# Stores of the last group in fewer transfers over two queues, and sums and weightings moved behind a bank's read, in a fused linear-attention and SwiGLU kernel

## The chip, the cores and the metric

The kernel runs on one core of one Trainium2 chip. The metric is the device time of one execution in microseconds (us), the median over several runs. A profile is one execution with the hardware profiler on; its "span" runs from the first to the last instruction and is about 2 us shorter than the device time. The record gives each run a state, fast or slow; all runs named here were fast, so like is compared with like.

## The reference

Eight batch entries of 576 tokens with eight heads of width 64 go through a linear attention, whose output (4608 tokens of width 512) goes through a gated feed-forward layer of inner width 1536.

```python
def _attn_ref(q, k, v):                      # q, k, v: (8, 8, 576, 64)
    theta = pi / 2 * arange(S) / S
    phi = lambda x: concatenate([relu(x) * cos(theta), relu(x) * sin(theta)], axis=-1)
    q_p, k_p = phi(q), phi(k)
    kv = einsum('bhsf,bhsd->bhfd', k_p, v)
    z = sum(k_p, axis=2)
    return einsum('bhsf,bhfd->bhsd', q_p, kv) / (einsum('bhsf,bhf->bhs', q_p, z)[..., None] + 1e-6)

def _moe_ref(x, w_gate, w_val, w_out):       # x: (4608, 512), weights 512x1536, 512x1536, 1536x512
    g = x @ w_gate
    return (g * sigmoid(g) * (x @ w_val)) @ w_out
```

## The kernel before

The 4608 tokens are worked in nine groups of 512. For each group TensorE runs 12 steps of the first two matmuls (line 531). Between them it makes the attention tiles of the next group, which are transposed by DMA into `xT`. From the third group on, the last matmul of a group is done as seven products on half-size blocks (Strassen's way), in `out_by_quarters`. Each product is 12 matmuls of 256 columns (line 640), and is added up in a "bank", a buffer of partial sums that VectorE or ScalarE reads (`a`, `b`, `c`, `e` in the code). Four token sums of the hidden tile (line 611) feed the products; weight differences were made once.

In this section code is cut; "# ..." marks a cut.

```python
def store(t, cols=slice(0, d_model), queues=None):          # two transfers, 64 partitions each
    for e in range(2):
        idx = 2 * t + e
        (queues or (nc.sync, nc.sync))[e].dma_start(out=out_v[idx // NC, idx % NC][:, cols],
                                                    in_=ob_of(t)[e * SH:(e + 1) * SH, cols])

def sums_behind(fc):                                         # token sums, some after each step
    for n, lo, hi in {7: ((3, 0, 4),), 8: ((1, 0, 4),), 9: ((2, 0, 4),), 10: ((4, 0, 4), (3, 4, 6)),
                      11: ((1, 4, 6), (2, 4, 6), (4, 4, 6))}.get(fc, ()):
        token_sum(n, lo, hi)

def phi_q(b, g):                                             # one "weighting": relu, then times a table
    # ...
    relu_op("act", o, o)                                                      # ScalarE, line 234
    nc.vector.tensor_tensor(out=st[b, "q"][:, g], in0=..., in1=tab, op=ALU.mult)   # VectorE, line 251

def out_by_quarters(tg, slot_of):
    # ... product(to, a, b, first) is 12 matmuls; added(o, ps, x) is VectorE: o = ps * DOWN + x  (line 647)
    product(a, aq[:, 0, 0], bq[:, 0, 0], True)               # 1st
    nc.scalar.mul(out=C12, in_=a[0], mul=DOWN)
    product(e, S3, T3, True)                                 # 2nd
    added(C22, e, C12)
    # ...
    slot_of(0)                                               # other work: a weighting
    product(b, S2, T2, True)                                 # 3rd, into bank b
    added(C21, b, C22)                                       # reads b
    product(a, aq[:, 1, 0], bq[:, 1, 0], False)              # 4th
    nc.scalar.mul(out=C11, in_=a[0], mul=DOWN)
    # ... last group: store C11
    slot_of(1)                                               # a weighting
    product(b, S1, T1, False)                                # 5th, adds onto bank b
    added(C22, b, C22)                                       # reads b
    # ... last group: store C22
    product(c, aq[:, 1, 1], T4, True)                        # 6th
    added(C21, c, C21)
    # ... store C21 (last group) or the two lower tiles
    slot_of(2)                                               # a weighting
    product(b, S4, bq[:, 1, 1], False)                       # 7th, adds onto bank b
    added(C12, b, C12)
    # ... store C12 (last group) or the two upper tiles
    slot_of(3)

def load_behind(b):                                          # GpSimd: loads start when phit has landed
    nc.gpsimd.tensor_copy(out=hold2, in_=phit[b - 1][0:1, :, 0, 0, 0])
    load(b, "q")
    if b > 3:
        load_kv(b)

# which slot takes which weighting (b > 3): four of q, then four of k and v; qturn_dma (SyncE) turns q into phit
fs, tq = [p0 + 11 + i for i in range(8)], (p0 + 15, p0 + 16)
```

## Time and profile before

| | before |
|---|---|
| device time, median of the first three runs | 323.78 us (323.49 to 324.77) |
| span of the profiled run | 321.0 us |
| TensorE busy | 309.1 us (96%) |
| holes (idle time) of TensorE at products, by its weight loads | 2.7 us, in four groups |
| the tail: last add to the output tile, to the end of the span | 7.5 us |

A line of the timeline gives the start in us, the duration in us, the engine, the source line, the operation and its tiles; in brackets stands how long the engine was idle just before, and what ended that. PE is TensorE's matmuls, PEld its weight loads, DVE VectorE, ACT ScalarE, POOL GpSimd; L640 is line 640 of the kernel. "SPq" and "ACTq" are DMA issues on the queues of SyncE and ScalarE. In a list of waits the numbers are the total in us, the count and the longest; "issue" there means that the profile names no cause. The prediction below shows the lines of this profile.

### The profile page before, as it was taken

How to read it: one execution, taken by the hardware profiler on the slowest of the kernel's cores; microseconds unless marked ns; L12 is line 12 of the kernel's file. 1: busy time of each engine (PE TensorE's matmuls, PEld its weight loads, DVE VectorE, ACT ScalarE, POOL GpSimd, SP SyncE). 2: the span in 40 equal slices, each digit the busy share in tenths (PEclk: the TensorE clock that was granted, in tenths of full speed). 3: DMA queues.
4: the chain of work that ended last, by engine and by line, in shares of the span. 5: the costliest groups of instructions: out<-in, count | busy, mean ns of one | idle time of the engine just before them, and what ended most of it. 6: DMA issues, size and time to landing. Idle time of an engine off the chain costs nothing.

```text
span 321.0 us, 6625 instructions
## 1 busy us (share of the span) xinstructions
PE 309.1 (96%) x2624; PEld 182.9 (57%) x2624; DVE 224.8 (70%) x448; ACT 130.1 (41%) x237; POOL 35.3 (11%) x60
## 2 busy tenths in 40 slices
PE   8899999999999989999999999999999999999990
PEld 4596555454445574558554855476547644854580
DVE  7873876788658888598859875888487448643750
ACT  7553556662436345334433543244431132223210
POOL 6755102010102000020003000300000000000000
PEclk9999999999999999999999999999999999999997
DMA  7999998988996956999696959597931411150014
GB/s 266 216 200 198 205 202 143 211 111 109 179 203 81 195 73 148 133 124 166 140 133 97 198 132 135 78 182 155 143 63 33 98 34 34 35 130 3 0 26 104
DMA packets 74862, 41.06 MB, mean 128 GB/s; under 512 B 50000, under 2 KB 69968, under 8 KB 74832
## 3 DMA queue, kind: packets, MB, share of 16 engines
q1 hardware_dynamic: 52480, 22.95, 40.2%
q0 software_dynamic: 22192, 17.57, 36.6%
q8 instruction: 20, 0.33, 0.4%
q10 hardware_dynamic: 160, 0.13, 0.2%
q14 instruction: 10, 0.08, 0.1%
HBM read 37.75 MB, written 9.44 MB: 147 GB/s over the span
## 4 chain that ended last, share of the span: by engine, by line
PE 75%; DVE 10%; DMA 5%; issue 3%; SPq 3%; ACT 2%; DVEq 0%; POOLq 0%; POOL 0%; ACTq 0%
PE banks L531 49%; PE banks L640 13%; PE banks L580 6%; DMA phit<-r_q 3%; PE banks L301 2%; DVE ob L647 2%; DMA raw_q<-in_q_dram 2%; DVE ht L542 2%; DVE sums L611 2%; PE banks L415 1%; SPq L570 1%; SPq L274 1%; DVE r_q L251 1%; PE banks L461 1%; PE banks L397 1%
## 5 line engine op out<-in xcount | busy, mean ns | idle before, releaser
L537 ACT ACTIVATE sg<-banks 128x512 bf16<-128x512 f32 (+2 forms) x116 | 65.8, 568 | 120.1 <-PE banks L531 113.1
L531 PE MATMUL banks<-xT,wv_sb 128*128 128x512 bf16 (+2 forms) x464 | 111.3, 364 | 0.0
L531 PE MATMUL banks<-xT,wg_sb 128*128 128x512 bf16 (+2 forms) x464 | 111.3, 364 | 0.0
L542 DVE TENSOR_TENSOR ht<-sg,banks 128x512 f16<-128x512 bf16 (+2 forms) x116 | 74.5, 648 | 51.7 <-PE banks L531 44.7
L531 PEld LDWEIGHTS <-wv_sb 128*128 128x128 bf16 x464 | 44.9, 98 | 48.7
L531 PEld LDWEIGHTS <-wg_sb 128*128 128x128 bf16 x464 | 43.1, 98 | 41.7 <-issue 0.2
L640 PEld LDWEIGHTS <-ht 128*128 128x128 f16 x336 | 32.4, 98 | 6.6 <-issue 2.7
L647 DVE SCALAR_TENSOR_TENSOR ob<-banks,ob 128x512 f32<-128x512 f32 (+1 forms) x38 | 24.5, 647 | 13.6 <-PE banks L640 13.5
L640 PEld LDWEIGHTS <-sums 128*128 128x128 f16 x252 | 24.6, 98 | 2.9
L255 DVE TENSOR_TENSOR v<-raw_v,tab 128x1152 bf16<-128x1152 bf16 x31 | 22.7, 752 | 0.2 <-ACT raw_v L691 0.2
L580 PE MATMUL banks<-wo_sb,ht 128*128 128x512 f16 x96 | 22.7, 379 | 0.0
L438 DVE TENSOR_TENSOR x<-banks,rec 128x512 bf16<-128x512 f32 (+1 forms) x32 | 21.6, 674 | 1.3 <-PE banks L397 0.3
L251 DVE TENSOR_TENSOR r_q<-raw_q,tab 128x1152 bf16<-128x1152 bf16 x24 | 17.9, 753 | 5.2 <-ACT raw_q L234 5.2
L640 PE MATMUL banks<-wt_sb,ht 128*128 128x256 f16 x168 | 19.5, 272 | 2.0 <-DVE ob L647 2.0
L640 PE MATMUL banks<-wo_sb,ht 128*128 128x256 f16 x168 | 20.6, 273 | 0.0
L640 PE MATMUL banks<-wt_sb,sums 128*128 128x256 f16 x168 | 19.5, 273 | 0.0
L234 ACT ACTIVATE raw_k<-raw_k 128x576 bf16<-128x576 bf16 (+1 forms) x25 | 17.0, 694 | 0.0
L234 ACT ACTIVATE raw_q<-raw_q 128x576 bf16<-128x576 bf16 x24 | 15.4, 675 | 2.5 <-DMA raw_q<-in_q_dram 2.5
L611 DVE TENSOR_TENSOR sums<-ht 128x1024 f16<-128x1024 f16 (+1 forms) x28 | 15.5, 553 | 0.2
L840 POOL COPY hold<-phit 1x2 bf16<-1x2 bf16 x5 | 0.9, 176 | 132.5 <-DMA phit<-r_q 132.5
L580 PEld LDWEIGHTS <-ht 128*128 128x128 f16 x96 | 9.1, 98 | 8.9 <-issue 0.2
L415 PEld LDWEIGHTS <-phit 128*128 128x128 bf16 (+1 forms) x240 | 10.0, 100 | 6.5 <-issue 1.3
(95 smaller groups left out, 210.5 us busy)
## 6 DMA issues: line engine op xcount, KB each, us to landing
out_dram<-ob SPq DMA_DIRECT2D x64, 128.0 KB, 2.4
raw_k<-in_k_dram POOLq DMA_DIRECT2D x7, 576.0 KB, 9.0
raw_q<-in_q_dram POOLq DMA_DIRECT2D x6, 576.0 KB, 6.6
raw_v<-in_v_dram POOLq DMA_DIRECT2D x6, 576.0 KB, 12.2
wo_sb<-in_moe_w_out_dram POOLq DMA_DIRECT2D x3, 512.0 KB, 12.8
wg_sb<-in_moe_w_gate_dram POOLq DMA_DIRECT2D x5, 256.0 KB, 9.0
wv_sb<-in_moe_w_val_dram POOLq DMA_DIRECT2D x5, 256.0 KB, 9.4
wo_sb<-in_v_dram SPq DMA_DIRECT2D x2, 576.0 KB, 4.1
```

The costliest lines, as they stand in the source:

```text
L234: nc.scalar.activation(out=out, in_=in_, func=AF.Relu)
L251: nc.vector.tensor_tensor(out=st[b, "q"][:, g], in0=o.unsqueeze(2).to_broadcast([P, NC, 2, D]), in1=tab, op=ALU.mult)
L255: nc.vector.tensor_tensor(out=v2s[b % 2][:, g, :, :, 0:D], in0=(first if b == 0 and g == 0 else {"v": raw_of(b, "v")})["v"][:, g].unsqueez ...
L415: nc.tensor.matmul(out=ps[ms, e, g * D1:(g + 1) * D1], lhsT=phit[b][:, e, g, c:c + n].rearrange("p c s -> p (c s)"), rhs=kv2s[b % 2][:, e, ...
L438: nc.vector.tensor_tensor(out=st["x", t].rearrange("p (y e d) -> p e y d", e=2, d=D)[:, :, ys], in0=ps[:, :, 0:2 * J * D1].rearrange("p e ...
L531: nc.tensor.matmul(out=st["f", tg, fc, lo][i], lhsT=(wg_sb, wv_sb)[i][:, kc, fs], rhs=xT[tg][:, ts, kc], start=(kc == 0), stop=(kc == KC - 1))
L537: nc.scalar.activation(out=sg[:, 0:n], in_=st["f", tg, fc, lo][0], func=AF.Silu, scale=DOWN)
L542: nc.vector.tensor_tensor(out=ht[:, fc, r:r + n], in0=st.pop(("s", tg, fc, lo))[:, 0:n], in1=ps[1], op=ALU.mult)
L580: nc.tensor.matmul(out=o_ps[t], lhsT=ht[:, fc, r:r + P], rhs=wo_sb[:, fc], start=(fc == 0), stop=(fc == FC - 1))
L611: nc.vector.tensor_tensor(out=o[:, lo:hi], in0=x[:, lo:hi], in1=y[:, lo:hi], op=op)
L640: nc.tensor.matmul(out=at_of(to, i), lhsT=a[:, kc, i * P:(i + 1) * P], rhs=b[:, kc], start=first and kc == 0 and (i == 0 or len(to) == 2), ...
L647: nc.vector.scalar_tensor_tensor(out=o[:, sl], in0=ps[i][:, 0:1] if len(ps) == 2 else ps[i], scalar=DOWN, in1=x[:, sl], op0=ALU.mult, op1= ...
```

## The change

It intends two things. In the last group, whose stores nothing hides, it makes fewer store instructions and shares them between SyncE and ScalarE. In the groups that also weight the next batch entry, it takes a token sum and two weightings out of VectorE's way ahead of the read that the fifth product waits for.

```diff
+    def store_two(t, cols):
+        for e in range(2):
+            (b, c), (b1, _) = divmod(2 * t + e, NC), divmod(2 * t + 2 + e, NC)
+            assert b == b1
+            (nc.sync, nc.scalar)[e].dma_start(
+                out=out_v[b, c:c + 3:2, :, cols].rearrange("c p f -> p c f"),
+                in_=obs[t // 2][e * SH:(e + 1) * SH, :, cols])
 # ... sums_behind
-                          11: ((1, 4, 6), (2, 4, 6), (4, 4, 6))}.get(fc, ()):
+                          11: ((1, 4, 6), (2, 4, 6))}.get(fc, ()):
 # ... out_by_quarters
-        slot_of(0)
         product(b, S2, T2, True)
         added(C21, b, C22)
+        token_sum(4, 4, 6)
+        slot_of(0)
         product(a, aq[:, 1, 0], bq[:, 1, 0], False)
 # ... the last group's first three quarters (one of them shown)
         if last:
-            for t in (t0, t0 + 1):
-                store(t, slice(0, HD))
+            store_two(t0, slice(0, HD))
 # ... the plan of the weightings
-            fs, tq = [p0 + 11 + i for i in range(8)], (p0 + 15, p0 + 16)
+            fs, tq = [p0 + 12, p0 + 12] + [p0 + 11 + i for i in range(2, 8)], (p0 + 15, p0 + 16)
```

The last quarter, C12, is stored as before in four 64 KB transfers, two on each queue.

More of the change, by code (lines that the diff above doesn't have):

```diff
@@ L671, in out_by_quarters @@
         if last:
-            for t in (t0 + 2, t0 + 3):
-                store(t, slice(HD, d_model))
+            store_two(t0 + 2, slice(HD, d_model))
         c = home("c")
@@ L677, in out_by_quarters @@
         free("c")
-        for t in (t0 + 2, t0 + 3):
-            store(t, slice(0, HD) if last else slice(0, d_model))
+        if last:
+            store_two(t0 + 2, slice(0, HD))
+        else:
+            for t in (t0 + 2, t0 + 3):
+                store(t)
         slot_of(2)
@@ L684, in out_by_quarters @@
         for t in (t0, t0 + 1):
-            store(t, slice(HD, d_model) if last else slice(0, d_model), (nc.sync, nc.scalar) if last else None)
+            store(t, *((slice(HD, d_model), (nc.sync, nc.scalar)) if last else ()))
         slot_of(3)
```

## The prediction

> **What bounds the kernel now.** I read the page's first two parts, then the lists of waits, then the timeline around the seven-product output of each group (line 640 is every product, line 647 the VectorE operation that adds a bank into the output tile, line 251 a weighting of q, line 611 a token sum), and last the timeline of the end.
>
> ```profile
> span 321.0 us, 6625 instructions
> PE 309.1 (96%) x2624; PEld 182.9 (57%) x2624; DVE 224.8 (70%) x448; ACT 130.1 (41%) x237; POOL 35.3 (11%) x60
> PE   8899999999999989999999999999999999999990
> ```
>
> TensorE is the bound: every slice is full but the last and the start. So only two things can pay: holes in TensorE's row, and the part after its last matmul. 321.0 less 309.1 is 11.9 us. The list of waits says where the holes lie (columns: total us, times, longest):
>
> ```profile
> PE banks L640 <- DVE ob L647: 2.0, 4, 0.9
> PEld L640 <- issue: 2.7, 4, 1.1
> ```
>
> There are four holes, all at products and all ended by VectorE. The weight-load row counts 2.7 us, since a matmul's modelled end hides some of the gap. In the timeline one such hole (fourth group) looks so:
>
> ```profile
> 145.85 0.42 DVE L611 TENSOR_TENSOR sums<-ht,sums 128x512 f16<-128x512 f16 x1
> 146.19 0.75 DVE L251 TENSOR_TENSOR r_q<-raw_q,tab 128x1152 bf16<-128x1152 bf16 x1
> ...
> 147.92 0.69 DVE L647 SCALAR_TENSOR_TENSOR ob<-banks,ob 128x512 f32<-128x512 f32 x1
> 148.07 1.47 PE L640 MATMUL banks<-wo_sb,ht 128*128 128x256 f16 x12
> 148.52 0.75 DVE L251 TENSOR_TENSOR r_q<-raw_q,tab 128x1152 bf16<-128x1152 bf16 x1
> 149.19 0.68 DVE L647 SCALAR_TENSOR_TENSOR ob<-banks,ob 128x512 f32<-128x512 f32 x1
> 149.58 0.60 ACT L663 ACTIVATE ob<-banks 128x512 f32<-128x512 f32 x1 [2.76 <-PE banks L640]
> 149.93 2.78 PE L640 MATMUL banks<-wt_sb,ht 128*128 128x256 f16 x24 [0.39 <-DVE ob L647]
> 150.07 1.25 ACT L234 ACTIVATE raw_q<-raw_q 128x576 bf16<-128x576 bf16 x2
> 150.78 0.76 DVE L251 TENSOR_TENSOR r_q<-raw_q,tab 128x1152 bf16<-128x1152 bf16 x1 [0.90 <-ACT raw_q L234]
> 151.45 0.68 DVE L647 SCALAR_TENSOR_TENSOR ob<-banks,ob 128x512 f32<-128x512 f32 x1
> 152.54 1.47 PE L640 MATMUL banks<-wo_sb,sums 128*128 128x256 f16 x12
> ```
>
> The fourth product starts at 148.07. The fifth adds onto the bank that VectorE's read at 149.19 has yet to take out, and starts at 149.93, when that read ends. VectorE is late because a token sum and two weightings stand ahead of it. The end of the kernel:
>
> ```profile
> 309.16 0.60 ACT L663 ACTIVATE ob<-banks 128x512 f32<-128x512 f32 x1 [3.33 <-PE banks L640]
> 309.78 8.79 SPq L570 DMA_DIRECT2D out_dram<-ob  x14
> 311.58 1.47 PE L640 MATMUL banks<-wo_sb,sums 128*128 128x256 f16 x12
> 312.93 1.44 ACTq L570 DMA_DIRECT2D out_dram<-ob  x2
> 313.09 0.42 DVE L647 SCALAR_TENSOR_TENSOR ob<-banks,ob 128x256 f32<-128x256 f32 x1 [0.23 <-PE banks L640]
> ```
>
> The results are complete at 313.51 (313.09 + 0.42), but SyncE is still issuing its 14 stores until 318.57, one every 8.79 / 14 = 0.63 us. The last one starts at 318.0 and takes 2.0 us from issue to landing (median of these 14), so 320.0; the span ends 1.0 us later. The tail is bound by one queue's issuing.
>
> **What the Trainium skill says.** (1) "Perfetto Trace Analysis", section "What 'DMA-bound' means": a kernel can be bound by the issuing engine's sequencer, seen as a solid row of DMA slices there. The trace agrees: 14 issues without a hole while the DMA engines are at 0.28 to 0.75 of their time in each microsecond from 313 to 320. (2) "DMA: Bandwidth & Descriptors", section "Issuing engines are not separate DMA queues": issuing from several engines saves only the sequencer's time for issuing. Here that time is the bound, so it is just what counts. (3) Same page, "Anatomy of one DMA": about 2.0 us fixed per DMA, mostly the receipt of the write. The trace has 1.9 to 2.3 us for the last 16 stores. (The page fitted it for another issuing path; the trace's figure is the one I use.) (4) "PSUM — Partial Sum Buffer", "The four PSUM rules": a synchronised read of a partial sum in the midst of accumulation is allowed. That is what the bank does between third and fifth product, and the wait at 149.93 is the synchronisation.
>
> **The change, part by part.** TensorE's instruction order is the same; only VectorE, ScalarE and the stores differ. (I compared the built orders.)
>
> *Stores.* Last group: 16 transfers of 64 KB become six of 128 KB and four of 64 KB, half on each queue, so SyncE issues 5 and not 14. Nothing is saved in bytes. When do they go out, if nothing before the tail moved? First pair at 309.78, second at 310.9 (after the add at 310.47), third pair after the add at 311.78, which takes about 0.6: 312.4. The last four need the two adds that end at 312.9 and 313.51. At 0.6 us an issue: 312.4 to 313.0, 313.0 to 313.65, 313.65 to 314.3 on SyncE. ScalarE's two old issues take 0.55 and 0.79 (1.44 in all with a gap), so there I have the last start at 313.7 to 313.8. Is a doubled transfer dearer to issue? The first loads of the run, on SyncE, have 128 rows of two pieces each and take 0.44 to 0.51 us to issue, so I take no more than 0.6 to 0.7. Landing: 2.0 on SyncE, 2.3 on ScalarE (its median). I add 0.1 because 512 KB now leave within 1.3 us; at 179 GB/s with a share of 0.75 (microsecond 314 to 315) full rate is about 240 GB/s, so 512 KB need 2.1 us of the engines and the last pieces queue a little. So landing at about 316.1 and not 320.0: **minus 3.9 us** (3.6 to 4.2).
>
> *Moved work.* One token sum (0.42) and two weightings (0.75 each, 0.67 from start to start) leave the place before the third bank's read; a third weighting was behind it already. Only the groups that carry weightings (the four with holes) gain. Without the hole the fifth product starts 1.31 after the fourth (246.84 to 248.15 in a later group without weightings), so the holes are: 117.18 − 114.79 − 1.31 = 1.08; 149.93 − 148.07 − 1.31 = 0.55; and by the same sum 0.51 and 0.53. Together 2.67, the 2.7 of the list. But the work does not vanish. In the new order VectorE has, for the fourth group: read of the third product at 148.27 (0.20 after its end) to 148.87, token sum to 149.29, two weightings to 150.63. The third weighting still needs ScalarE's relu at 150.07, which waits for ScalarE's copy of the fourth product: it starts at 150.78 as before. Then the read after the fifth product starts at 151.45, as before, and ends at 152.13. The **seventh** product adds onto that bank too. TensorE would reach it at 148.07 + 3 × 1.31 = 152.00 and waits until 152.19. So a new wait of 0.19 remains, and the group gains 152.54 − 152.19 = 0.35, not 0.55. The same sum gives 0.88 for the first such group (read 118.17 to 118.86, seventh at 118.92 for 119.80), then 0.31 and 0.32. Sum: **minus 1.86 us**. The rest of the run is full on TensorE, so it reaches the end.
>
> Total 3.9 + 1.86 = 5.8; 323.78 − 5.8 = **318.0 us**, 1.8% less.
>
> **The rivals.** *A: the moved work comes back entire at the seventh product.* For it: three weightings stand in a row. Against: the last is paced by ScalarE as before. It would leave the tail alone: 319.9. *B: no wait comes back,* as when products run a bit later or the adds release sooner: 2.67 and 3.9 give 317.2, the only way past 2%. *C: the tail becomes bound by DMA bandwidth or by dearer issues.* Two 128 KB transfers at a time at 240 GB/s need 1.1 us a quarter and quarters come 1.1 to 1.5 us apart, so it is near the limit; if the two-piece stores took 1.2 us each to issue, the last landing moves by about 0.6 and the total to 318.6. *D: later weightings delay the transposes and loads behind them.* The last weighting of a group comes no later than before, so I see nothing.
>
> **Range and chances.** Tail 3.4 to 4.3, moved work 1.2 to 2.7, runs that scatter by some 0.5 us (323.49 to 324.77 before): 316.9 to 319.3. Faster by over 2% needs 6.5 us, nearly the whole of B with the best tail: 0.2. Slower has no mechanism: 0.01.
>
> **What would show it.** In the new profile: five store issues on each of SyncE and ScalarE; last store issued about 2.2 us before landing and within 0.4 us of the last add; last add to span's end about 3.6 us (7.5 before). No wait at the fifth product; four waits of about 0.2 us at the seventh. Last matmul about 1.9 us earlier. Wrong if the seventh waits as long as the fifth did, if a two-piece store takes over 1 us to issue, or if landing takes over 3 us.

## The result and the profile after

| | before | after |
|---|---|---|
| device time, median (lowest to highest), four runs each | 323.63 (323.12 to 324.77) us | 318.36 (318.19 to 318.71) us |
| ratio | | 0.983, 95% interval 0.981 to 0.986 |
| span of the profiled run | 321.0 us | 316.5 us |
| holes of TensorE at products | 2.7 us | 0.8 us |
| idle time of TensorE before the sixth group, by its weight loads | 0.2 us | 0.8 us |
| last add to the end of the span | 7.5 us | 4.2 us |

A ratio is the mean time of one kernel's fast runs over that of the other's in the same rounds, so it is not quite the ratio of the medians. The device time fell by 5.3 us, where 5.8 were predicted.

The page's first lines after:

```profile
span 316.5 us, 6619 instructions
PE 308.6 (98%) x2624; PEld 182.7 (58%) x2624; DVE 225.0 (71%) x448; ACT 130.1 (41%) x237; POOL 35.7 (11%) x60
PE   8899999999999999999999999999999999999994
```

Busy times hardly changed (TensorE 308.6 us for 309.1); TensorE's share rose since the span shrank around it, and the last slice now holds work. From the list of waits after (line 640 has become 648):

```profile
PEld L648 <- issue: 0.8, 4, 0.2
PEld L531 <- issue: 0.8, 1, 0.8
PE banks L531 <- DMA xT<-x: 0.6, 1, 0.6
```

The four holes at products are down from 1.1 at most to 0.2 each. (A wait in the start-up, at L372, is also longer, 0.8 us for 0.2; the first group with a gain still starts its products only 0.05 us later.) A wait for a DMA has come up: once, TensorE comes to a group's first step and the transposed input has not landed. The fourth group's products in the timeline after (line 647 is now 655, 611 is 619, 663 is 672):

```profile
147.23 1.47 PE L648 MATMUL banks<-wo_sb,ht 128*128 128x256 f16 x12
147.43 0.69 DVE L655 SCALAR_TENSOR_TENSOR ob<-banks,ob 128x512 f32<-128x512 f32 x1 [0.56 <-PE banks L648]
148.04 0.41 DVE L619 TENSOR_TENSOR sums<-ht,sums 128x512 f16<-128x512 f16 x1
148.37 1.42 DVE L251 TENSOR_TENSOR r_q<-raw_q,tab 128x1152 bf16<-128x1152 bf16 x2
148.54 2.78 PE L648 MATMUL banks<-wt_sb,ht 128*128 128x256 f16 x24
148.74 0.60 ACT L672 ACTIVATE ob<-banks 128x512 f32<-128x512 f32 x1 [2.19 <-PE banks L648]
149.24 1.25 ACT L234 ACTIVATE raw_q<-raw_q 128x576 bf16<-128x576 bf16 x2
149.94 0.76 DVE L251 TENSOR_TENSOR r_q<-raw_q,tab 128x1152 bf16<-128x1152 bf16 x1 [0.15 <-ACT raw_q L234]
150.62 1.43 DVE L655 SCALAR_TENSOR_TENSOR ob<-banks,ob 128x512 f32<-128x512 f32 x2
151.36 1.47 PE L648 MATMUL banks<-wo_sb,sums 128*128 128x256 f16 x12
```

The fourth product starts at 147.23, and the fifth at 148.54, 1.31 later and without a hole: VectorE now reads the bank at 147.43, at once. The sum and two weightings come after that read. The third weighting waits for ScalarE's relu, and the next read of the bank starts only at 150.62. The seventh product starts at 151.36, 2.82 after the fifth, where 2.62 would be free of waiting: the 0.2 us that are left.

Where the new wait shows, at the start of the sixth group:

```profile
183.98 1.47 PE L648 MATMUL banks<-wo_sb,sums 128*128 128x256 f16 x12
185.98 0.56 PEld L531 LDWEIGHTS <-wg_sb 128*128 128x128 bf16 x4 [0.82 <-issue]
186.01 1.02 PE L531 MATMUL banks<-xT,wg_sb 128*128 128x512 bf16 x4 [0.56 <-DMA xT<-x]
```

And the same place in the kernel before:

```profile
186.90 0.56 PEld L531 LDWEIGHTS <-wg_sb 128*128 128x128 bf16 x4 [0.23 <-issue]
```

After the change the group's last transpose was issued at 178.61, 2.4 us earlier than before (181.0), since VectorE reaches that tile sooner. But it took 7.3 us to land where it had taken 5.8, and landed at 185.88. In the kernel before it landed at 186.79. In both kernels the first weight load of the group starts 0.10 us after the landing, so TensorE waited for this transpose before the change too: 0.2 us, where the other groups from the fourth on start with 0.01 us of idle time. The list of waits of before has it as `PEld L531 <- issue: 0.2, 1, 0.2`, with no DMA named, and the prediction passed over it.

The tail after:

```profile
308.54 3.31 SPq L577 DMA_DIRECT2D out_dram<-ob  x3
308.54 3.35 ACTq L577 DMA_DIRECT2D out_dram<-ob  x3
...
311.84 0.42 DVE L655 SCALAR_TENSOR_TENSOR ob<-banks,ob 128x256 f32<-128x256 f32 x1 [0.23 <-PE banks L648]
311.94 1.20 SPq L570 DMA_DIRECT2D out_dram<-ob  x2
311.99 1.44 ACTq L570 DMA_DIRECT2D out_dram<-ob  x2
```

Both queues issue at the same times. The output is complete at 312.26 (311.84 + 0.42), and the last issue starts at 312.87 on ScalarE, 0.6 us later; on the one queue before it started 4.5 us after the last add.

### The profile page after: what moved, and what is told of

The parts are those of the page before. It is cut to its first block, busy times and chain, and to the rows that moved or that the text cites. A ratio compares the mean times of both kernels' runs of the same rounds, so it can differ in the third digit from the quotient of the medians.

```text
span 316.5 us, 6619 instructions
## 1 busy us (share of the span) xinstructions
PE 308.6 (98%) x2624; PEld 182.7 (58%) x2624; DVE 225.0 (71%) x448; ACT 130.1 (41%) x237; POOL 35.7 (11%) x60
## 4 chain that ended last, share of the span: by engine, by line
PE 92%; DMA 2%; DVE 2%; ACT 2%; issue 0%; ACTq 0%
PE banks L531 59%; PE banks L648 18%; PE banks L588 6%; PE banks L301 3%; PE banks L415 2%; DMA xT<-x 2%; PE banks L461 1%; PE banks L397 1%; DVE v L255 1%; PE banks L168 1%; PE banks L341 0%; PE banks L503 0%; ACT L200 0%; ACT phit L349 0%; ACT kvd L313 0%
## 5 line engine op out<-in xcount | busy, mean ns | idle before, releaser
L531 PE MATMUL banks<-xT,wg_sb 128*128 128x512 bf16 (+2 forms) x464 | 111.3, 364 | 0.6 <-DMA xT<-x 0.6
L531 PE MATMUL banks<-xT,wv_sb 128*128 128x512 bf16 (+2 forms) x464 | 111.3, 364 | 0.0
L531 PEld LDWEIGHTS <-wv_sb 128*128 128x128 bf16 x464 | 44.9, 98 | 48.7
L531 PEld LDWEIGHTS <-wg_sb 128*128 128x128 bf16 x464 | 43.1, 98 | 42.3 <-issue 0.8
```

Of the source, the lines that this page charges most:

```text
L531: nc.tensor.matmul(out=st["f", tg, fc, lo][i], lhsT=(wg_sb, wv_sb)[i][:, kc, fs], rhs=xT[tg][:, ts, kc], start=(kc == 0), stop=(kc == KC - 1))
```

## The experiments

The theory: the tail was bound by SyncE's issuing, and the moved work takes away the holes at the fifth product but runs into two later limits, a small one at the seventh product and the landing of the transposes of x. The rivals: merging rather than the second queue shortens the tail; the wait for the transpose is chance; what is gained ahead of a wait is not lost in it. All results were correct.

| run | time, us | ratio (95% interval) | span | last add to end |
|---|---|---|---|---|
| after_again | 318.21 | 0.984 (0.982 to 0.986) | 317.1 | 4.2 |
| stores_only | 320.15 | 0.990 (0.988 to 0.992) | 318.5 | 4.1 |
| moves_only | 321.77 | 0.995 (0.993 to 0.997) | 319.7 | 7.5 |
| two_queues_64k | 318.44 | 0.984 (0.982 to 0.986) | 316.6 | 4.1 |
| one_queue_128k | 319.87 | 0.989 (0.987 to 0.990) | 317.8 | 5.5 |
| third_later | 318.72 | 0.984 (0.982 to 0.986) | 317.1 | 4.1 |
| pairs_all | 317.29 | 0.981 (0.979 to 0.983) | 315.5 | 4.0 |
| pairs_third | 316.88 | 0.979 (0.978 to 0.981) | 315.4 | 4.0 |
| pairs_third_again | 316.80 | 0.978 (0.976 to 0.980) | 315.0 | 4.0 |
| last_merged | 316.90 | 0.979 (0.977 to 0.981) | 315.3 | 4.2 |

The kernel before had medians of 323.41 us (11 runs, the first four rows), 323.64 (9 runs, the next four) and 323.84 (9 runs, the last two).

### The changed kernel again

> The changed kernel once more, as the measure for the others of this call. Both theories: about 318.3 us (0.984 of before). What it is to tell: whether the new wait of TensorE for the transpose of x (0.7 to 0.8 us at the start of the sixth group) belongs to the kernel or was chance. If it belongs: 0.6 to 0.9 us again in the same place, last add to end of the span 4.2 us. If chance: no such wait and a span of 315.7.

The wait came again, in the same place: 1.3 us of TensorE's idle time before the sixth group. So it is not chance, but its size is not steady. Of the runs below that have the moved work and, in the earlier groups, the stores of before, each has such a wait too: 0.3 us in moves_only and in two_queues_64k, at the start of the fifth group, 0.4 us in one_queue_128k, at the start of the seventh, and three in third_later. By the weight loads TensorE is idle before the sixth group in all six of these runs (0.3 to 1.6 us), and not in stores_only (0.01 us).

### The stores alone

Edit: from the changed kernel, the moved work back in its old places.

```diff
-                          11: ((1, 4, 6), (2, 4, 6))}.get(fc, ()):
+                          11: ((1, 4, 6), (2, 4, 6), (4, 4, 6))}.get(fc, ()):
+        slot_of(0)
         product(b, S2, T2, True)
         added(C21, b, C22)
-        token_sum(4, 4, 6)
-        slot_of(0)
-            fs, tq = [p0 + 12, p0 + 12] + [p0 + 11 + i for i in range(2, 8)], (p0 + 15, p0 + 16)
+            fs, tq = [p0 + 11 + i for i in range(8)], (p0 + 15, p0 + 16)
```

> Only the stores changed; token sum and weightings in their old places. My theory: the two parts don't touch, so the tail alone comes back: last add to end 4.2 us for 7.5, four holes of 2.7 us in all still at the fifth product, no wait for the transpose; 323.6 - 3.3 = 320.3 us, ratio 0.990. Rival: if the stores owe part of their gain to the earlier end of the last group, under 2.5 us.

The time fell by 3.3 us and the tail by 3.4, as the theory had it. The holes at the fifth product were 3.5 us by the weight loads in this run, one of them 1.4: there the q that is to be weighted landed late (ScalarE stood idle for it 2.4 us, until 146.55), and in the old order that weighting stands ahead of the read.

### The moves alone

Edit: from the kernel before, the same lines as above the other way round, with the stores of before.

> Only the moved sum and weightings; the stores of before. My theory: holes at products go from 2.7 to 0.8 us, a wait of about 0.7 us for the transpose of x comes up in the sixth group, so the last matmul comes 1.2 us earlier, tail 7.5 as before: 322.4 us, ratio 0.996. Rival (the wait for the transpose is from the stores or chance): no such wait, 321.7 us.

The time fell by 1.6 us (321.77 for 323.41), between the two forecasts. The holes at products were 0.8 us and the tail 7.5, as expected; the wait for the transpose was 0.3 us and in the fifth group (by the weight loads 0.6 us there and 0.3 before the sixth), so smaller and not where it was expected. The two parts alone give 3.3 + 1.6 = 4.9 us of the 5.2 that the whole gave: within the scatter they add up.

### Two queues, not merged; merged, one queue

Edit for two_queues_64k: `store_two` issues its two rows as separate 64 KB transfers.

```diff
-            (nc.sync, nc.scalar)[e].dma_start(out=out_v[b, c:c + 3:2, :, cols]..., in_=obs[t // 2][e * SH:(e + 1) * SH, :, cols])
+            for i in range(2):
+                b, c = divmod(2 * (t + i) + e, NC)
+                (nc.sync, nc.scalar)[e].dma_start(out=out_v[b, c][:, cols], in_=obs[t // 2][e * SH:(e + 1) * SH, i, cols])
```

> The changed kernel, but the merged stores of the last group split again into 64 KB transfers, eight on each queue. Theory A (one queue's issuing was the limit, two queues remove it, and merging adds little): last store issued within 1 us of the last add, tail 4.0 to 4.6 us, time within 0.3 us of the changed kernel. Theory B (the number of transfers matters): each queue falls behind by two issues, last issue about 1.3 us later, tail 5.3 us, time about 319.4 us.

Edit for one_queue_128k: the merged stores and the last four all go to SyncE.

```diff
-            (nc.sync, nc.scalar)[e].dma_start(
+            nc.sync.dma_start(
-            store(t, *((slice(HD, d_model), (nc.sync, nc.scalar)) if last else ()))
+            store(t, *((slice(HD, d_model),) if last else ()))
```

> The changed kernel with its merged stores of the last group all on SyncE (ten issues on one queue). Theory A (one queue's issuing is the limit of the tail): the last four issues follow two of the third quarter at 0.6 us each, so the last starts about 1.9 us after the last add and not 0.6, tail 5.4 us for 4.2, time 319.5 us. Theory B (merging alone did it): tail 4.2 to 4.5 us, time 318.3 us.

Without merging but over two queues the time was 318.44 us, the changed kernel's within the scatter. The last issue came 1.1 us after the last add and not 0.6, but its 64 KB landed in 2.0 us and the span ended 1.0 us later (2.3 and 1.4 us in the changed kernel). With merging on one queue it was 319.87 us. The end of that kernel's timeline:

```profile
311.86 0.42 DVE L655 SCALAR_TENSOR_TENSOR ob<-banks,ob 128x256 f32<-128x256 f32 x1 [0.23 <-PE banks L648]
312.63 2.48 SPq L570 DMA_DIRECT2D out_dram<-ob  x4
```

The last four issues take SyncE from 312.63 to 315.11, 2.8 us beyond the last add at 312.28. So one queue's issuing time sets the tail: merging, with all ten issues on one queue (before: fourteen there and two on ScalarE's), leaves 5.5 us of 7.5, and sharing between two queues takes it to 4.1 or 4.2 with or without merging.

### The third weighting later

Edit: one more weighting goes behind the read after the fifth product.

```diff
-            fs, tq = [p0 + 12, p0 + 12] + [p0 + 11 + i for i in range(2, 8)], (p0 + 15, p0 + 16)
+            fs, tq = [p0 + 12, p0 + 12, p0 + 14] + [p0 + 11 + i for i in range(3, 8)], (p0 + 15, p0 + 16)
```

> The changed kernel with the third weighting of a group (and its relu) moved behind the read after the fifth product. My theory: the four waits of 0.2 us at the seventh product go (0.8 us to under 0.1), but TensorE then reaches the next group earlier and waits longer for the transpose of x that lands with the burst of loads: that wait grows from 0.3-1.3 us by about 0.5. Net: 318.0 us, no clear gain. Rival: the gain reaches the end in full, 317.5 us.

The holes at products were gone. TensorE's waits in the later two thirds of that run:

```profile
152.99 1.04 PE L531 MATMUL banks<-xT,wg_sb 128*128 128x512 bf16 x4 [0.42 <-DMA xT<-x]
185.99 1.02 PE L531 MATMUL banks<-xT,wg_sb 128*128 128x512 bf16 x4 [0.40 <-DMA xT<-x]
219.10 1.02 PE L531 MATMUL banks<-xT,wg_sb 128*128 128x512 bf16 x4 [0.75 <-DMA xT<-x]
```

Instead of one wait for a transpose there are three, 1.6 us in all, and the time is no lower (ratio 0.984, as after_again had). The 0.8 us saved at the products came back at the next limit.

### The stores of the other groups merged too

Edit: in the third to the eighth group, two tiles' rows go out in one transfer where both rows lie in the same batch entry, still on SyncE.

```diff
+    def store_pair(t):
+        for e in range(2):
+            (b, c), (b1, c1) = divmod(2 * t + e, NC), divmod(2 * t + 2 + e, NC)
+            if b == b1:
+                nc.sync.dma_start(out=out_v[b, c:c + 3:2].rearrange("c p f -> p c f"),
+                                  in_=obs[t // 2][e * SH:(e + 1) * SH])
+            else:
+                # two transfers as before
 # ... in out_by_quarters, where the group is not the last
-            for t in (t0 + 2, t0 + 3):
-                store(t)
+            store_pair(t0 + 2)
```

> The changed kernel with the stores of the other groups merged too where both rows lie in one batch entry, still on SyncE: four to six issues a group for eight. Theory A (the transpose of x is late since the loads that share the DMA engines start when the transposes of q land, and those stand behind the stores in SyncE's queue): transposes of q issued about 2 us earlier, loads earlier, the wait for the transpose of x gone, 317.6 us. Theory B (that wait comes from the transpose's own length, or chance): still 0.3 to 1.3 us somewhere, 318.3 us.

Why a store may matter for a transpose of x: SyncE issues, in this order, a group's stores, then the transposes of the weighted q into `phit` (line 274). When these have landed, GpSimd starts the loads of the next q, k and v (`load_behind`), and the last transposes of x of the next group are in flight beside those loads. SyncE's queue in the fourth group of the changed kernel:

```profile
152.08 6.01 SPq L570 DMA_DIRECT2D out_dram<-ob  x8
158.20 8.12 SPq L274 DMA_TRANSPOSE phit<-r_q  x2
```

And in pairs_all (line 585 has the merged stores, 589 the others):

```profile
152.06 3.12 SPq L585 DMA_DIRECT2D out_dram<-ob  x3
155.24 1.30 SPq L589 DMA_DIRECT2D out_dram<-ob  x2
156.66 8.41 SPq L274 DMA_TRANSPOSE phit<-r_q  x2
```

The transposes of q are issued 1.5 us earlier. GpSimd's release comes at 169.23 for 170.53. The transpose of x that was late is issued at 178.6 as before, lands in 6.4 us for 7.3, and TensorE waits for no transpose anywhere. The time is 317.29 us, about 1 us less than the changed kernel had (the intervals of the ratios, 0.979 to 0.983 and 0.982 to 0.986, just overlap). It was run at another time. Merging made no difference in the tail, where two queues had room, and made this one in the midst of the run.

### Both together, and the last quarter merged

pairs_third is third_later's edit on top of pairs_all; pairs_third_again is the same kernel once more.

> Both edits of this call together. If theory A of each holds, the gains add since nothing is left to wait for: holes at products under 0.1 us, no wait for a transpose, last matmul 1.5 us earlier than in the changed kernel, 316.8 us, ratio 0.979. If the transpose's wait is not lifted by the merged stores: 318.0 us.

> The same kernel as pairs_third, as the measure for last_merged and to see whether its gain stands: 316.9 us, ratio 0.979, no wait of TensorE for a transpose over 0.3 us, last add to end of the span 4.1 to 4.3 us.

Now the third weighting's later place pays: 316.88 and 316.80 us. In pairs_third there is no hole at a product and one wait of 0.3 us, at the sixth group's start; in its repeat the list has none. Their intervals (0.978 to 0.981 and 0.976 to 0.980) lie below that of the changed kernel (0.982 to 0.986). This version beats both kernels. The difference from pairs_all alone is 0.4 us; the intervals of the two ratios overlap, but in the call that had both, each of the four runs of pairs_third (316.60 to 317.17 us) lies below each of the five of pairs_all (317.25 to 317.57). The next limit is near: in all four runs with merged stores, last_merged included, the sixth group starts 0.06 to 0.15 us after its transpose has landed.

last_merged stores the last quarter of pairs_third as two transfers of 128 KB after the last add.

```diff
-            for t in (t0, t0 + 1):
-                store(t, slice(HD, d_model), (nc.sync, nc.scalar))
+            store_two(t0, slice(HD, d_model))
```

> pairs_third with the last four 64 KB stores as two of 128 KB after the last add. In the changed kernel ScalarE's first of the four takes 0.79 us to issue, so its second starts 0.6 us after the last add. Theory A (that late issue is the part of the tail that I had too small): issue 0.1 us after the last add, landing 2.6 to 2.9 us for a two-piece store, tail 3.9 us for 4.2, about 316.6 us. Theory B (the landing grows by as much, since 256 KB start at once): tail 4.2 to 4.4 us, no gain.

The issues started right after the last add (at 311.17 and 311.18 us, the add ended at 311.14), but landed in 2.8 and 3.0 us (the last store of pairs_third_again: 2.2), and the tail was 4.2 us for 4.0. TensorE also had a wait of 0.2 us for a transpose, before the seventh group. The time did not move. So the issue that comes 0.6 us late in the changed kernel is no reserve: what is gained in issuing is lost in landing.

## Why the prediction was right or wrong

**What binds, and the size of the whole.** TensorE's row and the one queue's tail bound the kernel, as said; 318.36 us lies in the range, 0.4 above the predicted time. The two terms were each too large: in the profiles the tail gave 3.25 us and not 3.9, the moves 1.25 and not 1.86 (last add at 312.26 for 313.51), together 4.5. The device times show more, 5.3, mostly because the profiled run of before was a quick one (323.03 us, 0.6 below the median). About 0.3 us lies outside the spans (device time less span is 2.1 us before and 1.8 after) and stays unexplained. Two sums of the prediction are slightly off without consequence: 512 KB at 240 GB/s take 2.2 us and not 2.1, and its two ranges make 316.8 to 319.2 us.

**The tail.** The mechanism is shown by one_queue_128k and two_queues_64k. Mis-sized were two terms. The last issue starts 0.61 us after the last add and not 0.25, because ScalarE's first of the last two issues took 0.79 us. The landing of the last store (2.3 us, where 2.4 was taken) was right. From landing to the end of the span it took 1.4 us in this run, where I had kept the 1.0 of before; it is 0.9 to 1.0 in the three profiles without two-piece stores in the last group and 1.0 to 1.4 in the nine with them, and I can't say why. The dearer issue of a two-piece store (rival C) did not come: 0.60 to 0.74 us. Their landing did lengthen, 2.5 to 3.0 us (one took 3.02, just past the 3 us that were named as a sign of being wrong, but it was not among the last), and last_merged shows that this takes back what fewer issues give.

**The moved work, up to the seventh product.** This step held closely. The holes at products went from 2.7 to 0.8 us, so 1.9 us, where 1.86 was worked out. Group by group, TensorE's first product of the groups after the first and the second gain came 0.84 and 1.19 us earlier than before, from a start 0.05 us later: gains of 0.89 and 0.35 for the 0.88 and 0.35 forecast. Rival A (all of it back at the seventh product) was wrong: 0.2 us a group came back. Rival B (nothing back) was wrong too.

**The sentence that failed.** "The rest of the run is full on TensorE, so it reaches the end", and in rival D "The last weighting of a group comes no later than before, so I see nothing". At the next group's products the lead was 0.92 us and not 1.50: 0.6 us went into the wait for the transpose of x. Rival D looked for later transposes; but this one landed 0.91 us earlier, and TensorE came 1.50 us earlier. As the group started on the transpose's landing in both kernels, only the 0.91 could pass. That the wait is from the order of SyncE's queue and the loads behind it is supported by pairs_all, which takes it away, and by third_later, where more lead turns into more of that wait. pairs_all also has fewer transfers in flight, and no run changes one without the other. The traces speak for the loads: from GpSimd's release of the loads to the landing of the sixth group's transpose it takes 15.4 to 16.2 us in all twelve profiles (15.7 to 16.0 with merged stores, so no shorter), while from the transpose's own issue it takes 5.6 to 8.0. That is a correlation and not a test. Why the fifth or the seventh group has a wait as well in some runs stays open.

## What to carry to other kernels

When a hole is closed on the bounding engine, ask what the engine will meet sooner: look at when each input of the next stage lands, and not only at the list of waits. Here an input was already 0.2 us late, and its line named no cause. At the end of a kernel, count issues per queue times the time of one issue (here 14 times 0.63 us). Here a second queue removed the backlog, while merging on two queues moved time from issuing into landing. In the midst of the run merging paid, since something else waited behind the stores in the same queue.

## What the Trainium skill lacked or had wrong

- "DMA: Bandwidth & Descriptors", section "Issuing engines are not separate DMA queues", says the sequencer time saved by several issuing engines "is usually small relative to the DMA itself". Here, with 64 KB stores at 0.63 us an issue, 14 issues took 8.8 us, while a store lands in 2.0 us; the second queue took the tail from 5.5 us (one queue, merged) to 4.2.
- No page gives the time of one issue on SyncE or ScalarE by the size of the transfer (the page above has one count of sequencer cycles, for "previous generations", with no size). For the stores of the last group the runs show 0.47 to 0.65 us on SyncE and 0.55 to 0.80 on ScalarE; earlier in the run a few took up to 2.0. It hardly grows from 64 KB in 64 pieces (0.54 to 0.60 on SyncE) to 128 KB in 128 pieces (0.60 to 0.65).
- The same page gives about 2.0 us as the fixed cost, for DMAs issued by GpSimd ("Anatomy of one DMA"). Stores of 64 KB from SyncE and ScalarE landed in 1.9 to 2.3 us in the kernel before, and in 2.3 to 2.7 behind the two-piece stores of the changed kernel; these, of 128 KB and issued in pairs, took 2.5 to 3.0.
- The same page's section "DMA Transpose (X-bar)" has no latency of a transpose beside other traffic. One 128x512 transpose landed in 2.4 us at best and in 4 to 11 us beside the loads of q, k and v, and that spread decided 0.3 to 1.6 us of this kernel.
